# Score matmuls over all 128 rows of the key tile instead of 64

## The chip, the cores and the metric

The kernel runs on one core of a Trainium2 chip. TensorE multiplies matrices; VectorE, ScalarE and GpSimd work on what it leaves in PSUM and on SBUF; SyncE and the others issue DMAs. The metric is device time in microseconds, here the median of the runs of the kernel. A matmul has a stationary operand, which a weight load puts into the 128 by 128 array (rows are the contraction, columns the outputs), and a moving operand, which streams through it. In the profile PE is the matmuls, PEld the weight loads, DVE VectorE, ACT ScalarE, POOL GpSimd and SP SyncE.

## The reference

Attention with pooled keys and values, then a feed-forward layer with a maximum over three products.

```python
# q, k, v: (8, 8, 576, 64): batch, heads, sequence, head size
k_p = k.reshape(B, H, 72, 8, D).mean(axis=3)
v_p = v.reshape(B, H, 72, 8, D).mean(axis=3)
scores = q @ k_p^T / sqrt(D)              # 576 x 72 a head
attn = exp(scores - max); attn = attn / (attn.sum() + 1e-9)
x = (attn @ v_p), heads side by side      # 4608 x 512
h = maximum(maximum(x @ w1, x @ w2), x @ w3)   # 4608 x 768
out = h @ w_out                           # 4608 x 512
```

The change touches only the product of queries and pooled keys.

## The kernel before

The eight batches flow through the kernel as a pipeline: while the feed-forward layer works on the tokens of one batch, the attention of a later one is made. Tokens are taken 512 at a time by the feed-forward layer (stage n is tokens 512n to 512n + 511) and 576 at a time by a batch of the attention.

Feed-forward. The kernel uses max(a, b, c) = a + max(0, b - a, c - a): it subtracts w1 from w2 and w3 once, makes the two products x(w2 - w1) and x(w3 - w1) (`hidden_part`, line 362, tile `pw`), takes the relu of the first on ScalarE (line 368) and the maximum with the second on VectorE (line 370), and adds x(w1 w_out) to the output (`project`, lines 412 and 416, tile `po`). Each `pw` is four matmuls of 512 columns. Later stages make such products with seven instead of eight block products (`seven`, line 789; `out_seven`, line 713).

Attention of a batch b. GpSimd adds groups of eight keys and values (lines 161 to 164). Queries are transposed, on TensorE (`turn_q`, line 192) or by a DMA (step `T`, line 302), into `qTs[b]`, a tile of 128 rows: a block of 128 columns of the queries holds two groups of the 64 head dimensions, so the even group lies in rows 0 to 63 and the odd one in rows 64 to 127. The pooled keys are transposed too (`keys`, line 199), and lines 208 to 211 copy them twice: into `kz_all[b % 2][0]`, where they fill rows 0 to 63, and into `kz_all[b % 2][1]`, where they fill rows 64 to 127. The other 64 rows of both tiles are zero from memsets at the start (lines 142 and 319). VectorE makes these copies, and ScalarE those of `kz_all[..][1]` for batches above 2.

`score` (line 213) multiplies one head's keys with a strip of its queries; `f % 2` says whether the strip lies in the upper or the lower rows, and picks the matching key tile. `scores` (line 228) makes a head of batches 1 to 6 with two such calls: 320 columns into one PSUM bank and 256 into the next. Since `tp` differs by one, one of the two has the upper rows and the other the lower. An exponential on ScalarE (line 223) then reads both. The PSUM tile has two buffers, so the scores of one head wait for the exponential two heads before. Batch 0 (`scores4`, `scores2`) and batch 7 (`scores_flat`) cut the strips differently; there `len(pools)` is 1 and 3.

The order of the work on each engine is the order of the calls, written by hand. `block(0, ...)` (line 810) sets batch 1 among the first stage: slots 26 to 30 hold its scores, alone or two heads together. `MIDDLE` (line 881) is the order of stages 1 to 4 and holds the scores of batches 2 to 5, such as "h s0 h s1 h s2": `h` is one `pw` of four matmuls, `s0` the scores of head 0. `LEAD` (line 531) does the same for batch 6, and `ORDER` (line 846) for batch 7. `v0` to `v4` in these strings are the products with the values (line 268) for 128 tokens each, `x0` to `x4` the transposes of their results, `k` the key copies.

Lines 215 to 220 are the ones to follow:

Of the kernel before, what the change touches and what calls it, by code (L numbers as in the profile page):

```python
# [14 lines left out]
def kernel(  # L15
# [44 lines left out]
    pools = [first.enter_context(tc.tile_pool(name="ps0", bufs=1, space=PSUM))]  # L60
# [152 lines left out]
    def score(b, h, out, tp, i0, i1):  # L213

        f = NG * (h // 2) + tp
        n = f // 2
        rows = slice(0, 128) if len(pools) != 2 else slice(64 * (f % 2), 64 * (f % 2) + 64)
        nc.tensor.matmul(out, kz_all[b % 2][f % 2][rows, h, :],  # L218
                         qTs[b][rows, n + i0:n + i1, 64 * (h % 2):64 * (h % 2) + 64],
                         start=True, stop=True)  # L220
# [7 lines left out]
    def scores(b, h):  # L228
        psc = psum([128, 1024], F32, name="psc", tag="att", bufs=2)
        score(b, h, psc[:, 192:512], 0, 0, 5)  # L230
        score(b, h, psc[:, 512:768], 1, 0, 4)
        exp(ets[b][:, h, :], psc[0:Sp, 192:768])

    def scores_flat(b, j):

        psc = psum([128, 512], F32, name="psf", tag=SC[0], bufs=SC[1])
        u = 8 * j
        while u < 8 * j + 8:
            h, t = divmod(u, NG)
            tp, i0 = divmod(t, 5)  # L240
            n = min(5 - tp - i0, 8 * j + 8 - u)
            at = 64 * (u - 8 * j)
            score(b, h, psc[:, at:at + 64 * n], tp, i0, i0 + n)
            u += n
        exp(ets[b].rearrange("p h s -> p (h s)")[:, 512 * j:512 * j + 512], psc[0:Sp])
# [734 lines left out]
```

## Time and profile before

| | before |
|---|---|
| time, median of 3 runs | 230.57 us (230.28 to 230.62) |
| span of the profiled execution | 228.6 us |
| TensorE matmuls busy | 219.2 us, 96% |
| weight loads busy | 138.6 us, 61% |
| VectorE busy | 149.1 us, 65% |
| ScalarE busy | 122.3 us, 53% |
| GpSimd busy | 138.7 us, 61% |

The page gives the profiled execution by its span alone, from the first to the last instruction; the times of the runs are those of the whole execution on the device. Matmuls are pipelined: one starts while the last columns of another are still on their way, and the end of each is modelled. So the sum of their durations is not what they cost; the distance from one start to the next is. The mean granted clock of TensorE is 0.998 of full speed.

In a line of a group, "64*128" is the part of the array in use (rows by columns), "64x320 bf16" the operand, then the count, the busy time, the mean duration in ns, and the idle time just before, with what ended it. In the timeline the first column is the start and the second the duration of a merged group, both in us.

### The profile page before, as it was taken

Reading aid. Unit: us, or ns where it says so; the run is one execution under the profiler, and the core shown is the slowest. Engines: PE = TensorE matmul, PEld = TensorE weight load, DVE = VectorE, ACT = ScalarE, POOL = GpSimd, SP = SyncE. Lnnn points to the kernel's source line nnn. Section 1 sums busy time; section 2 is a strip of 40 time slices with the busy share of each in tenths; the row PEclk is TensorE's granted clock in tenths of the full one; section 3 lists DMA queues with packets and bytes.
Section 4 is the critical chain, followed back from the end, with each engine's and each line's share of the span. In section 5 each row is a group of like instructions: output and inputs, shape, how many; then the busy total and the mean of one; then the engine's idle time right before and its main releaser. Section 6 shows DMA issues by size and latency. Waiting matters only on the chain.

```text
span 228.6 us, 4690 instructions
## 1 busy us (share of the span) xinstructions
PE 219.2 (96%) x1806; PEld 138.6 (61%) x1807; DVE 149.1 (65%) x292; ACT 122.3 (53%) x221; POOL 138.7 (61%) x111
## 2 busy tenths in 40 slices
PE   7788999999999999999999999899999999999993
PEld 2477745369436533973396349534678677788882
DVE  3668875048465374876487558635668896898841
ACT  2277425746864477237623762575587545555330
POOL 7975202999959766687668755999600923773020
PEclk9999999999999999999999999999999999999999
DMA  6999999999569999359999996761351434200265
GB/s 181 211 196 196 212 203 208 192 189 221 107 106 212 224 211 199 61 123 164 220 205 168 167 250 113 155 171 51 50 128 26 106 67 106 46 3 0 47 208 163
DMA packets 47351, 33.54 MB, mean 147 GB/s; under 512 B 27041, under 2 KB 42337, under 8 KB 47329
## 3 DMA queue, kind: packets, MB, share of 16 engines
q0 software_dynamic: 16944, 16.98, 45.6%
q1 hardware_dynamic: 29936, 15.87, 29.7%
q10 hardware_dynamic: 448, 0.39, 0.7%
q8 instruction: 14, 0.23, 0.4%
q14 instruction: 9, 0.07, 0.1%
HBM read 34.60 MB, written 9.44 MB: 193 GB/s over the span
## 4 chain that ended last, share of the span: by engine, by line
PE 88%; DMA 4%; DVE 3%; ACT 2%; issue 1%; SPq 0%; ACTq 0%
PE pw L362 28%; PE po L416 9%; PE oA L713 9%; PE pA L789 7%; PE po L412 6%; PE psc L218 5%; PE oC L713 4%; PE pav L268 4%; PE pC L789 3%; DMA ktTrue<-in_k_dram 3%; PE oB L713 2%; PE pm L349 2%; PE pqt L192 2%; PE pB L789 2%; PE pxt L259 2%; DMA xT<-xn 1%
## 5 line engine op out<-in xcount | busy, mean ns | idle before, releaser
L362 PE MATMUL pw<-xT,mw 128*128 128x512 f16 (+1 forms) x336 | 73.1, 350 | 0.3 <-ACT xT L262 0.2
L370 DVE TENSOR_TENSOR hT<-t,pw 128x512 f16<-128x512 f16 (+1 forms) x42 | 25.5, 610 | 27.4 <-PE pw L362 25.0
L362 PEld LDWEIGHTS <-mw 128*128 128x128 f16 x336 | 28.6, 97 | 23.9 <-issue 0.6
L223 ACT ACTIVATE et<-psc 72x576 f16<-72x576 f32 (+2 forms) x54 | 35.1, 661 | 8.4 <-PE psc L218 8.2
L161 POOL TENSOR_TENSOR half<-vt 72x2048 f32<-72x2048 f16 x7 | 28.4, 4059 | 13.3 <-DMA vt<-in_v_dram 12.8
L162 POOL TENSOR_TENSOR half<-half 72x1024 f32<-72x1024 f32 (+1 forms) x13 | 27.2, 2096 | 12.2 <-DVE rcp L274 7.3
L368 ACT ACTIVATE t<-pw 128x512 f16<-128x512 f32 (+1 forms) x42 | 22.5, 537 | 16.6 <-PE pw L362 16.1
L276 DVE TENSOR_TENSOR xn<-pav,rcp 128x512 f16<-128x512 f32 x40 | 27.7, 692 | 1.4
L416 PE MATMUL po<-mwo,hT 128*128 128x512 f16 (+1 forms) x102 | 23.5, 367 | 0.0
L161 POOL TENSOR_TENSOR half<-ktFalse 96x1536 f32<-96x1536 f16 x6 | 18.8, 3128 | 5.2 <-issue 5.1
L218 PEld LDWEIGHTS <-kz 64*128 64x128 bf16 (+1 forms) x143 | 8.4, 94 | 21.7 <-issue 17.8
L564 POOL TENSOR_TENSOR pad<-xT 128x256 f16<-128x256 f16 x8 | 6.7, 835 | 21.4 <-ACT pad L795 13.4
L795 ACT CAST pad<-pA 128x512 f16<-128x512 f32 x27 | 15.6, 588 | 7.2 <-PE pA L789 7.0
L218 PE MATMUL psc<-qT,kz 64*128 64x320 bf16 (+3 forms) x120 | 17.7, 283 | 1.2 <-DVE qT L194 0.9
L274 DVE RECIPROCAL rcp<-pav 128x8 f32<-128x8 f32 x40 | 8.1, 203 | 14.9 <-PE pav L268 14.6
L723 ACT COPY osb<-oA 128x512 f32<-128x512 f32 x12 | 7.0, 586 | 19.5 <-PE oA L713 19.5
L268 PEld LDWEIGHTS <-et 72*128 72x128 f16 x320 | 15.2, 98 | 3.5 <-issue 0.2
L412 PE MATMUL po<-wm,xT 128*128 128x512 f16 (+1 forms) x68 | 16.6, 367 | 0.0
L268 PE MATMUL pav<-vp,et 72*128 72x65 f16 x320 | 16.4, 194 | 0.1
L769 DVE SCALAR_TENSOR_TENSOR hT<-pad 128x512 f16<-128x512 f16 x18 | 14.6, 825 | 2.1 <-ACT pad L799 1.7
L421 ACT COPY osb<-po 128x512 f32<-128x512 f32 (+1 forms) x16 | 9.2, 573 | 12.3 <-PE po L416 11.6
L789 PEld LDWEIGHTS <-sw 128*128 128x128 f16 x144 | 13.7, 98 | 2.4
(122 smaller groups left out, 377.8 us busy)
## 6 DMA issues: line engine op xcount, KB each, us to landing
out_dram<-osb SPq DMA_DIRECT2D x38, 128.0 KB, 5.2
ktFalse<-in_k_dram POOLq DMA_DIRECT2D x7, 576.0 KB, 6.9
qb<-in_q_dram POOLq DMA_DIRECT2D x7, 576.0 KB, 10.4
vt<-in_v_dram POOLq DMA_DIRECT2D x7, 576.0 KB, 14.6
mw<-in_moe_w_dram POOLq DMA_DIRECT2D x9, 256.0 KB, 9.3
out_dram<-osb SPq DMA_DIRECT2D x8, 256.0 KB, 5.9
ktTrue<-in_k_dram SPq DMA_DIRECT2D x3, 384.0 KB, 4.9
out_dram<-ob SPq DMA_DIRECT2D x8, 128.0 KB, 2.7
```

Source lines behind the costliest of these rows:

```text
L161: yield e.tensor_tensor(out=f, in0=t[:, :, 0:4, :], in1=t[:, :, 4:8, :], op=ALU.add)
L162: yield e.tensor_tensor(out=f[:, :, 0:2, :], in0=f[:, :, 0:2, :], in1=f[:, :, 2:4, :], op=ALU.add)
L218: nc.tensor.matmul(out, kz_all[b % 2][f % 2][rows, h, :], qTs[b][rows, n + i0:n + i1, 64 * (h % 2):64 * (h % 2) + 64], start=True, stop=True)
L223: nc.scalar.activation(out=out, in_=in_, func=FT.Exp, scale=1.0 / 64.0)
L268: nc.tensor.matmul(pav[:, h // 4, 65 * (h % 4):65 * (h % 4) + 65], ets[b][:, h, c0:c0 + 128], vp_all[:, b, h, :], start=True, stop=True)
L276: nc.vector.tensor_tensor(out=xn, in0=pv[:, :, :, 0:D], in1=rcp.to_broadcast([128, 2, 4, D]), op=ALU.mult)
L362: mm = nc.tensor.matmul(pw, w_sb[wi][:, kc, bass.ts(jc, 128)], x[:, kc], start=(kc == 0), stop=(kc == KCH - 1))
L370: nc.vector.tensor_tensor(out=hT[:, jc, c0:c1], in0=t, in1=pw, op=ALU.max)
L412: nc.tensor.matmul(po, tokens(128 * m, 128 * m + 128)[:, kc], wm_sb[:, kc, c], start=(kc == 0), stop=False)
L416: nc.tensor.matmul(po, hT[:, jc, bass.ts(mm, 128)], wo_sb[:, jc, c], start=False, stop=(jc == JCH - 1))
L713: nc.tensor.matmul(p, left, right, stop=(r == 4), skip_group_check=True, start=(i in FIRST and r == 0 and (m == 0 or n == LAST)))
L789: mm = nc.tensor.matmul(p[:, w], a[:, kc, bass.ts(g, 128)], b[:, kc, :], start=(i in FIRST and w + kc == 0), stop=(w + kc == 2), skip_grou ...
```

## The change

`rows` in `score` is the range of partitions that the matmul reads of both operands. Before, it is all 128 for batches 0 and 7 and the 64 rows that hold the head for batches 1 to 6. After, it is all 128 for every batch. The 64 rows that come in hold zeros in the key tile, so the products are the same.

```diff
         f = NG * (h // 2) + tp
         n = f // 2
-        rows = slice(0, 128) if len(pools) != 2 else slice(64 * (f % 2), 64 * (f % 2) + 64)
+        rows = slice(0, 128)
         nc.tensor.matmul(out, kz_all[b % 2][f % 2][rows, h, :],
                          qTs[b][rows, n + i0:n + i1, 64 * (h % 2):64 * (h % 2) + 64],
                          start=True, stop=True)
```

## The prediction

> **What bounds the kernel now.** I read the page first, for the bound, then its groups for the edited line, then the timeline of TensorE around those matmuls, then the same line where it already works with all 128 rows.
>
> ```profile
> span 228.6 us, 4690 instructions
> PE 219.2 (96%) x1806; PEld 138.6 (61%) x1807; DVE 149.1 (65%) x292; ACT 122.3 (53%) x221; POOL 138.7 (61%) x111
> PE 88%; DMA 4%; DVE 3%; ACT 2%; issue 1%; SPq 0%; ACTq 0%
> L218 PEld LDWEIGHTS <-kz 64*128 64x128 bf16 (+1 forms) x143 | 8.4, 94 | 21.7 <-issue 17.8
> ```
>
> TensorE is busy for 96% of the span and makes 88% of the chain that ended last, so a shorter TensorE stream is worth its length unless something else takes over. The last line is the clue: the weight loads of line 218 are the only frequent ones before which the loader idles long and for no work that the profile names. The same form by shape, all of TensorE:
>
> ```profile
> L218 PE MATMUL psc<-qT,kz 64*128 64x320 bf16 x48 | 14.3, 306 | 0.2 <-ACT et L223 0.2
> L218 PE MATMUL psc<-qT,kz 64*128 64x256 bf16 x48 | 13.1, 279 | 0.2 <-ACT kz L208 0.2
> ```
>
> So 96 matmuls change, 48 pairs (six batches, eight heads). They wait for nearly nothing. Their durations say little, as matmuls overlap; what a pair costs is the distance between starts. Timeline of TensorE, starts in the first column:
>
> ```profile
> 61.30 0.31 PE L218 MATMUL psc<-qT,kz 64*128 64x320 bf16 x2
> 61.54 1.04 PE L362 MATMUL pw<-xT,mw 128*128 128x512 f16 x4
> 62.51 0.31 PE L218 MATMUL psc<-qT,kz 64*128 64x320 bf16 x2
> 62.75 1.04 PE L362 MATMUL pw<-xT,mw 128*128 128x512 f16 x4
> 63.72 0.31 PE L218 MATMUL psc<-qT,kz 64*128 64x320 bf16 x2
> ```
>
> Two things are to be seen. Two matmuls together take 0.31 us, no longer than one of them (306 ns): the two halves of the array work at the same time. And four 512-column matmuls stand between, which need less than the time given to them. Their own pace, without scores, is in the chain in order of time:
>
> ```profile
> 101.65 2.59 PE pw L362 x12
> ```
>
> 2.59 / 12 = 0.216 us each, four 0.863. The period from one pair to the next is 62.51 - 61.30 = 1.21 (1.208 over 61.30 to 66.14), so a pair really costs 1.208 - 0.863 = 0.345 us. At 0.43 ns a column (0.44 us for 1024 columns, next fence) its longer half needs only 0.14 us. Of the rest, about 0.10 lies ahead (61.54 + 0.863 = 62.40, but the pair starts at 62.51) and 0.11 behind (62.51 + 0.14 = 62.65, but the next starts at 62.75): the array empties when it goes to 64 rows and again when it comes back.
>
> The batches whose scores already use 128 rows:
>
> ```profile
> 168.81 0.60 PE L218 MATMUL psf<-qT,kz 128*128 128x256 bf16 x5
> 169.25 0.42 PE L268 MATMUL pav<-vp,et 72*128 72x65 f16 x8
> ...
> 171.69 0.38 PE L218 MATMUL psf<-qT,kz 128*128 128x256 bf16 x2
> 171.91 0.60 PE L789 MATMUL pA<-pad,sw 128*128 128x256 f16 x4
> ```
>
> Five matmuls with 256 + 256 + 64 + 256 + 192 = 1024 columns take 169.25 - 168.81 = 0.44 us from start to start, two of 256 take 0.22: 0.43 ns a column, between neighbours of other types, with nothing lost ahead or behind. (The 72-row matmuls of line 268 follow without loss too, so it is not any count under 128 that empties the array.)
>
> **The change part by part.** Only the row range moves. No instruction is added or removed and no queue is touched; the keys' other 64 rows are zeros written once by the memsets of lines 142 and 319, done before 30 us, so the wider read adds no late wait; both halves of the query tile are written by the same copies or the same DMA transpose.
>
> *Lost: the two halves no longer overlap.* 320 + 256 = 576 columns at 0.43 ns are 0.247 us in place of 0.14 us: 0.107 us a pair, 48 x 0.107 = 5.1 us if nothing came back.
>
> *Gained: both gaps go.* 0.10 + 0.11 a pair. Net 0.345 - 0.247 = 0.098, called 0.10, a gain. The full-row pair is bounded by 0.247 (batch 7's pace) and, if one weight load of 97 ns a pair stood bare, 0.344, which is no gain at all; I take 0.247, because the rows of 168.81 are the same line, type and width, and there even a 64-column matmul hides the next load.
>
> The row of 61.30 agrees with a rule of the Trainium skill, page "TensorEngine Tiling (Array Packing)", section "Key Properties": a change of the tiling mode, other than of the tile, drains TensorE. Against the change speaks the page "TensorE: Matmul & The Clock Gate", Part 3, "What picks the tile position" and the goals behind it: matmuls of few rows in different row groups run concurrently, and one of them alone takes as long as one of 128 rows. This trace agrees with both; by the second alone the change would lose the 5.1 us, by both it wins 0.10 us a pair.
>
> *Sum.* Batches 2 to 6 have 40 pairs. 39 stand alone between 128-row matmuls as at 61.30: 3.9 us. At 147.2 the second half of batch 6's first pair waits for a copy of the keys on ScalarE until 147.69; there only the gap behind it goes, 0.11. Batch 1, 38 to 47 us, is different. Its first pair too waits for a key copy (VectorE, to 38.80) and gains the gap behind, 0.11; s3 at 42.02 is a lone pair, 0.10; s1 with s2 and s4 with s5 are issued as four matmuls that overlap and pay the gaps once, 0.46 us against 2 x 0.247 = 0.49: a loss of 0.03 each at most; for s6 and s7 the latter waits for ScalarE's exponential, and 0.11 behind it is won. Sum for batch 1: 0.11 + 0.10 - 0.06 + 0.11 = 0.26. All: 3.9 + 0.11 + 0.26 = 4.3 us.
>
> *Does it reach the end?* From 157 us to the last matmul TensorE has no gap of note, so what is won before is a plain shift. Before, ScalarE could be late next: in a stretch of scores it does two exponentials of 0.65 and one relu of 0.60, 1.90 us in two periods of 2.42, which become 2.22: 0.32 left. An exponential ends some 1.25 us after its pair starts, and its buffer is wanted two periods on: 2.42 before, 2.22 after. VectorE's slack is larger (5.1 of 9.2 us busy from 103.8 to 113.0). POOL runs without a break from 139.36 to 164.18; its keys of batch 7 are ready at 156.27 and read at 160.34, 4.1 us of cover against 4.2 us won by then. If POOL did not move, 0.1 us would be lost; it was released at 139.36 by VectorE, which moves too. Loads are issued some 20 us ahead of their use. I cost all this at nothing, and keep 1 us for it in the range. The short waits outside the scores (by the distance of starts 0.3 us each at 98.3, 120.8, 143.3, and 0.6 at 145.0) are for ScalarE or VectorE right behind TensorE's own work, and move along.
>
> The profiled execution has a span of 228.6 us; the median of the runs is 230.57, 2.0 above, which I take for the work around the span and leave alone. 228.6 - 4.3 = 224.3, and with 2.0 again **226.3 us**.
>
> **The rivals.**
> Slower: *the gaps stay and the halves come one after the other.* If the gaps came from the score's own start (its waits, the type change, the buffer) and not from the row count, each pair would cost 0.345 + 0.107 and the kernel 230.6 + 5.1 = 235.7 us. The point that decides is 0.107 us: more than half of the 0.21 us of gaps would have to remain. For it: most of these pairs carry a wait on ScalarE. Against: batch 7's scores carry such waits too and lose nothing, and the gap has one size at pairs with and without waits. The page's second rule above leads here if the drain is overlooked. 5 in 100.
>
> *A weight load stands bare* (the upper bound above): 0.344 a pair, nothing won, 230.5 us. For it: the loader idles 0.42 us before each of these loads today. Against: the same line hides its loads at 168.81. 2 in 100.
>
> *Half is absorbed.* ScalarE, POOL or a transfer paces a few stages: DMA engines are full in the stretches 81.0 to 90.6 and 126.5 to 135.7 (share 1.13 and 1.10), and POOL's cover at 160 us is as long as the gain. With half of 4.3 lost, 228.4. Against: TensorE waits there for none of them, and POOL idles 1 to 3 us several times a stage until 139 us. 11 in 100.
>
> *More comes than I count*: the shifted stages shorten the waits of 0.3 to 0.6 us named above, together 1.5 us; half of that gives 225.5. 5 in 100.
>
> **How the numbers follow.** The forecast, 226.3 within half a microsecond or so, has 77 in 100. Its own working gives 225.9 to 226.7 (0.09 to 0.11 a pair); absorbed waits of up to 1 us lift the end to 227.4, and a little less waiting lowers the other to 225.6. Left out are the slower case, the bare load, most of the absorbed case and part of the last, near 2 in 10. About 0.2% (0.46 us) is what measurements of this kernel can tell from no change, as its three runs span 0.34. Faster by more: 77 + 11 + 5 = 93, less one for an absorption that is almost whole, 92; within it, 3; slower, 5.
>
> **What the changed profile would show.** Right: line 218 has no 64*128 form left; the period of the score stretch falls from 1.21 to 1.11 us with the four matmuls between still at 0.863; the loader's idle time before line 218 shrinks from 17.8 us to little; the span is near 224.3. Wrong: a period that stays at 1.21 with a wait on ScalarE or VectorE ahead of the pair (absorbed), one of 1.31 with the 0.1 us gaps still there (slower), or new idle time of TensorE at 145 or 160 us for POOL or a transpose.

## The result, and the profile after

The changed kernel took 227.75 us (median of four executions, 226.4 to 228.01) against 230.52 before; the ratio is 0.9866, 95% interval 0.9836 to 0.9895. It is faster, but by 2.8 us where 4.3 were forecast, and above the stated range. The four executions were 228.01, 227.5, 226.4 and 228.0 us: one of them is the forecast, three are not. The profiled one is the slowest, with a span of 226.3 us. Its mean granted clock and those of the second and third are 1.0, that of the fourth is 0.992; by an estimate, 0.8% of its 226.2 us is up to 1.8 us, as much as it lost, so its loss need not be that of the profiled one.

Page of the changed kernel, span, busy time and chain, and its line 218:

```profile
span 226.3 us, 4691 instructions
PE 214.7 (95%) x1807; PEld 146.4 (65%) x1807; DVE 148.6 (66%) x292; ACT 122.3 (54%) x221; POOL 138.6 (61%) x111
PE 69%; DMA 15%; POOL 11%; issue 1%; DVE 1%; ACT 1%; POOLq 0%
L218 PEld LDWEIGHTS <-kz 128*128 128x128 bf16 x143 | 13.1, 98 | 13.3 <-ACT qT L194 1.1
L218 PE MATMUL psc<-qT,kz 128*128 128x320 bf16 x48 | 14.2, 299 | 0.1
```

Timeline of TensorE in the stretch that the prediction showed:

```profile
61.40 0.41 PE L218 MATMUL psc<-qT,kz 128*128 128x320 bf16 x2
61.65 1.03 PE L362 MATMUL pw<-xT,mw 128*128 128x512 f16 x4
62.51 0.41 PE L218 MATMUL psc<-qT,kz 128*128 128x320 bf16 x2
62.75 1.03 PE L362 MATMUL pw<-xT,mw 128*128 128x512 f16 x4
63.62 0.41 PE L218 MATMUL psc<-qT,kz 128*128 128x320 bf16 x2
```

The two matmuls of a pair now follow each other (0.41 us together instead of 0.31), and the next work starts 0.245 us behind the pair's start with nothing lost ahead. The period is 1.108 us instead of 1.208 (61.40 to 65.83, four periods): 0.100 us a pair, in all 32 pairs of batches 2 to 5. The weight loads of line 218 had 21.7 us of idle time before them, 17.8 without a named cause; they now have 13.3 (ahead of a pair 0.12 us instead of 0.42). TensorE did what was forecast. But the chain is now 69% TensorE instead of 88%, and DMA and GpSimd have 26%. Two pieces of the chain, start and length in us, show where it leaves TensorE:

```profile
54.43 1.00 POOL kp L164
138.71 6.32 DMA xT<-xn
```

From the first one back, the chain runs over GpSimd's sums of keys and values and the loads ahead of them, which is most of the 26%. The second one costs more. It is in the timeline of TensorE between batches 5 and 6, first before the change, then after:

```profile
145.56 0.82 PE L713 MATMUL oC<-mwo,tt 128*128 128x256 f16 x6
146.22 1.03 PE L362 MATMUL pw<-xT,mw 128*128 128x512 f16 x4
```

```profile
142.32 0.60 PE L713 MATMUL oC<-wm,tt 128*128 128x256 f16 x4
142.76 0.82 PE L713 MATMUL oC<-mwo,tt 128*128 128x256 f16 x6
145.17 1.02 PE L362 MATMUL pw<-xT,mw 128*128 128x512 f16 x4 [1.59 <-DMA xT<-xn]
```

Before, the product with `xT`, the transposed results of batch 5, follows the output matmuls at once. After, ten output matmuls start at 142.32 and need 1.09 us; the product could begin at 143.41 and begins at 145.17, 1.76 us late, when the DMA transpose has landed. The same matmuls stand one against the other in both traces, so the gain can be followed (start after, minus start of the same matmul before, in us; the three columns behind are other profiled executions of the unaltered changed kernel, further down):

| after | first shown | again | again2 | again3 |
|---|---|---|---|---|
| the common part, before any changed matmul (37.4) | +0.22 | +0.05 | +0.11 | +0.17 |
| the scores of batch 1 (51.1) | +0.09 | -0.08 | -0.02 | +0.04 |
| the key transposes of batch 2 (57.9) | +0.39 | -0.08 | -0.02 | +0.05 |
| the scores of batches 2 to 5 (135.4) | -2.80 | -3.27 | -3.21 | -3.15 |
| the wait for `xT` (146.2) | -1.05 | -3.27 | -3.22 | -3.15 |
| the scores of batch 6 (156.4) | -2.33 | -4.07 | -4.02 | -3.95 |
| the last matmul (224.5) | -2.34 | -4.03 | -3.98 | -3.92 |

Rows 2, 4 and 6, each against the row above it, are the change: 0.13, 3.2 and 0.80 us in every column but one. Rows 3 and 5 are data that came late in the execution shown first: 0.30 and 1.75 us. Its row 6 has 1.28 in place of 0.80, as batch 6's first pair, which used to wait for a copy of the keys, finds it done behind the long wait: that gives back 0.48, so the long wait costs 1.27 us net.

### The profile page after: what moved, and what is told of

Same layout as the page of the kernel before. It is cut to its first block, busy times and chain, and to the rows that moved or that the text cites. A ratio compares the mean times of both kernels' runs of the same rounds, so it can differ in the third digit from the quotient of the medians.

```text
span 226.3 us, 4691 instructions
## 1 busy us (share of the span) xinstructions
PE 214.7 (95%) x1807; PEld 146.4 (65%) x1807; DVE 148.6 (66%) x292; ACT 122.3 (54%) x221; POOL 138.6 (61%) x111
## 4 chain that ended last, share of the span: by engine, by line
PE 69%; DMA 15%; POOL 11%; issue 1%; DVE 1%; ACT 1%; POOLq 0%
PE pw L362 21%; PE oA L713 9%; DMA vt<-in_v_dram 8%; PE pA L789 7%; PE po L416 7%; PE po L412 5%; PE oC L713 4%; PE psc L218 4%; DMA mw<-in_moe_w_dram 4%; PE pC L789 3%; POOL half L161 3%; DMA xT<-xn 3%; PE pav L268 3%; PE oB L713 2%; POOL half L162 2%; PE pB L789 2%
## 5 line engine op out<-in xcount | busy, mean ns | idle before, releaser
L362 PEld LDWEIGHTS <-mw 128*128 128x128 f16 x336 | 31.6, 98 | 22.3 <-DMA xT<-xn 1.8
L370 DVE TENSOR_TENSOR hT<-t,pw 128x512 f16<-128x512 f16 (+1 forms) x42 | 25.4, 609 | 25.1 <-ACT et L223 17.8
L161 POOL TENSOR_TENSOR half<-vt 72x2048 f32<-72x2048 f16 x7 | 28.4, 4061 | 13.8 <-DMA vt<-in_v_dram 13.3
L218 PE MATMUL psc<-qT,kz 128*128 128x320 bf16 (+2 forms) x120 | 22.4, 278 | 0.8 <-DVE qT L194 0.6
L218 PEld LDWEIGHTS <-kz 128*128 128x128 bf16 x143 | 13.1, 98 | 13.3 <-ACT qT L194 1.1
L564 POOL TENSOR_TENSOR pad<-xT 128x256 f16<-128x256 f16 x8 | 5.9, 732 | 22.5 <-ACT pad L795 13.9
L766 DVE TENSOR_TENSOR pad<-pad,pC 128x512 f16<-128x512 f16 x18 | 12.3, 685 | 3.9 <-PE pC L789 3.6
```

The source lines that it names most:

```text
L161: yield e.tensor_tensor(out=f, in0=t[:, :, 0:4, :], in1=t[:, :, 4:8, :], op=ALU.add)
L218: nc.tensor.matmul(out, kz_all[b % 2][f % 2][rows, h, :], qTs[b][rows, n + i0:n + i1, 64 * (h % 2):64 * (h % 2) + 64], start=True, stop=True)
L362: mm = nc.tensor.matmul(pw, w_sb[wi][:, kc, bass.ts(jc, 128)], x[:, kc], start=(kc == 0), stop=(kc == KCH - 1))
L370: nc.vector.tensor_tensor(out=hT[:, jc, c0:c1], in0=t, in1=pw, op=ALU.max)
```

## The experiments

Two theories were open. A: the transpose is late because it shares the DMA engines with batch 7's loads, which the shorter stages have moved closer to it; how close differs from execution to execution. B: the transposes can't come earlier whatever TensorE does. And for the score pair itself: is it the change of the row mode that costs the 0.1 us twice, or the start of a score?

### The changed kernel once more

No edit.

> The changed kernel once more, unaltered. The profiled execution lost 1.76 us of its gain in one place: TensorE waits at 145.2 us for the transpose of batch 5's second 128 tokens (xT), which took 6.3 us to land where the kernel before had 3.2. Theory A (collision): that transpose shares the DMA engines with batch 7's loads and batch 7's query transpose, which the shorter stages have moved closer together; whether it is late differs from execution to execution. Then the runs spread from 226.3 (no wait) to 228.0, median 227 to 227.8, and the profile shows the wait at 145 in proportion to its time. Theory B (fixed floor): the transposes cannot come earlier whatever TensorE does; then all runs lie at 227.5 to 228.0. Both: each score pair costs 0.245 us.

Measured: 226.41 us (226.34, 226.17, 227.34, 226.47), ratio 0.9825 (0.9807 to 0.9844). Page and timeline of this execution:

```profile
span 224.6 us, 4690 instructions
PE 87%; DVE 4%; DMA 3%; ACT 2%; issue 1%; SPq 0%; ACTq 0%
...
142.29 0.82 PE L713 MATMUL oC<-mwo,tt 128*128 128x256 f16 x6
142.95 1.03 PE L362 MATMUL pw<-xT,mw 128*128 128x512 f16 x4
```

The product follows with no wait, and TensorE has its 87% back. B is out: the same program reaches 226.2 to 226.5. Two further sets of the unaltered kernel:

> The changed kernel unaltered, for more executions and a third profile. The two sets so far: 228.01, 227.5, 226.4, 228.0 and 226.34, 226.17, 227.34, 226.47. If the late transposes are a matter of chance in each execution, again a mix of 226.2 to 226.5 and of 227.2 to 228.0, with TensorE's wait at 145 us or elsewhere in the profile when the profiled one is slow, and no such wait when it is at 226.4.

> The changed kernel unaltered, beside the next two on one chip: a mix of 226.2 to 226.5 and of 227.0 to 228.0; median 226.4 to 227.

again2 gave 226.36, 227.08, 226.38, 227.02; again3 226.43, 226.23, 226.93, 226.33. All sixteen executions together: nine at 226.17 to 226.47, five at 226.93 to 227.50, two at 228.0; median 226.45. The kernel before lies at 230.1 to 231.0 beside them, with one of 232.0 among fifty-nine, whose granted clock was 0.991. The three profiled executions here were at 226.3 to 226.4, and have neither of the late rows of the table, as A expects.

### One half in the other row mode

The kernel before, with all 128 rows for the first matmul of each pair and 64 for the second:

```diff
-        rows = slice(0, 128) if len(pools) != 2 else slice(64 * (f % 2), 64 * (f % 2) + 64)
+        rows = slice(0, 128) if len(pools) != 2 or tp == 0 else slice(64 * (f % 2), 64 * (f % 2) + 64)
```

> The kernel before, with all 128 rows for the first matmul of each pair (320 columns) and 64 rows for the second (256 columns). Tells the price of the change of row mode apart from the overlap of the halves. If the 0.10 us ahead and behind belong to the change of row mode, a pair costs 0.136 + 0.10 + 0.107 + 0.10 + 0.01 = 0.45 us in place of 0.345, and the kernel gains nothing and loses 40 x 0.11 = 4 to 5 us: 234.5 to 235.5. If they belong to the start of a score (its wait, its type), the pair costs at most 0.35 and the time stays at 230.5.

Measured: 235.73 us (235.6 to 236.06), ratio 1.0224 (1.0211 to 1.0238), 5.0 us slower than the kernel before and 0.2 us above the range expected. Timeline of TensorE:

```profile
83.88 0.51 PE L218 MATMUL psc<-qT,kz 128*128 128x320 bf16 x2
84.32 1.04 PE L362 MATMUL pw<-xT,mw 128*128 128x512 f16 x4
85.19 0.51 PE L218 MATMUL psc<-qT,kz 128*128 128x320 bf16 x2
```

The period is 1.318 us and the pair costs 0.455 with the matmuls between at 0.863. By the starts nothing is lost ahead of the first, 128-row matmul, 0.096 is lost between the two, and 0.10 behind the 64-row one. So the gaps belong to the row mode and to no other trait of a score. Three ways of one pair then stand side by side: 64 and 64 rows 0.345, 128 and 64 rows 0.455, 128 and 128 rows 0.245 us.

### The change by parts

Batch 6 alone (`or b == 6` behind `len(pools) != 2`), and batches 1 to 5 alone (`or b < 6`):

> All 128 rows for batch 6 alone (from 147 us on), 64 for batches 1 to 5. Seven pairs at 0.10 and one at 0.11: 0.8 us less than the kernel before, 229.7 to 229.9, under every theory. Theory A (the shorter stages before 145 us bring transposes and loads together): the stages before 145 are as they were, so the spread stays that of the kernel before, 0.7 us or less. Theory C (the spread has nothing to do with those stages): a spread of 1 to 1.8 us here too.

> All 128 rows for batches 1 to 5, 64 for batch 6. Gains 32 x 0.10 + 0.1 to 0.2 = 3.4 us where no transpose is late: 227.2 to 227.3. Theory A: with the stages before 145 us shortened as in the changed kernel, some executions are 1 to 1.5 us slower, up to 228.7. Theory C: as much spread as in the run for batch 6 alone.

Measured: batch 6 alone 229.68 us (229.53 to 229.94) against 230.59 before, ratio 0.9962 (0.9949 to 0.9976): 0.9 us. Batches 1 to 5 alone 227.29 us (227.05 to 227.62), ratio 0.9856 (0.9843 to 0.987): 3.3 us. The parts add up to 4.2, what the undisturbed executions of the whole gain. Neither set had an execution more than 0.6 us above its fastest, so on the spread they don't decide between A and C.

### Which partner makes the transpose late

In the first, the query transpose of batch 7 is moved out of the stretch; in the second, the load of batch 7's values is left out, and batch 7 uses the values of batch 6 (its output is another). Lines of code that are cut end in "...".

```diff
-            1 v0 x0 2 v1 x1 7:T 6 7 v2 x2 5 v3 x3 v4 x4 3 6:k 4 v6+2 k7+3 v7+3
+            1 v0 x0 2 v1 x1 6 7 v2 x2 5 v3 x3 v4 x4 7:T 3 6:k 4 v6+2 k7+3 v7+3
```

```diff
-            h k k7< q7< v7< h a1 a3 a2 a4 ...
+            h k k7< q7< h a1 a3 a2 a4 ...
...
-                folding[what, b] = fold_steps(nc.gpsimd, vts[b], vp_all[:, b, :, 0:D])
+                folding[what, b] = fold_steps(nc.gpsimd, vts[min(b, 6)], vp_all[:, b, :, 0:D])
```

> The changed kernel with the DMA transpose of batch 7's queries put behind the five transposes of batch 5's values instead of between the second and the third. Theory A1 (the query transpose is the partner of the collision): the wait at 145 us goes, 226.3 to 226.6. Theory A2 (batch 7's loads are the partner): the wait stays, 227.5 to 228. Theory B: 227.5 to 228.

> The changed kernel without the load of batch 7's values (0.58 MB in SBUF); batch 7 uses those of batch 6, so this part of the output is another. Everything else is kept. Theory A2 (the loads are the partner): the loads end about 4 us earlier, before the transposes of batch 5 begin, the wait at 145 us goes, and every run is at 226.2 to 226.5, with little spread. Theory A1 or B: 227.5 to 228.

Measured: t7_late 226.86 us (226.57, 227.28, 226.02, 226.41, 227.95, 227.15), no_v7 226.42 us (226.42, 226.16, 227.75, 226.55, 226.3). As the unaltered kernel mostly isn't late either, these say little: both still have an execution near 227.8, so neither partner alone is behind all of the late ones. The way to decide is to make the suspected overlap certain:

```diff
-            h k k7< q7< v7< h a1 a3 a2 a4 f ! v5+2 h h s0 ...
+            h k h a1 a3 a2 a4 f ! v5+2 k7< q7< v7< h h s0 ...
```

> The changed kernel with batch 7's three loads issued behind the next fold step on GpSimd, about 7 us later, so that they are certain to run beside the transposes of batch 5 at 137 to 145 us. Theory A (a transpose beside a load is late): the wait at 145 us, which came in 1 of 4 profiled executions, is there in every one, 1 to 4 us long: 227.5 to 230. Rival (the wait was a chance stall that needs no load): 226.2 to 227.3 with a rare 228.

Measured: 227.45 us, all five executions at 227.12 to 227.59. A had expected 227.5 to 230 and its rival at most 227.3, so the times alone lie between the two. Timeline of TensorE:

```profile
142.37 0.82 PE L713 MATMUL oC<-mwo,tt 128*128 128x256 f16 x6
144.58 1.02 PE L362 MATMUL pw<-xT,mw 128*128 128x512 f16 x4 [1.39 <-DMA xT<-xn]
```

The same wait in the same place, 1.56 us by the starts, and a kernel 1 us slower than the unaltered one. The DMA packets of the traces (a packet is a piece in which a transfer is moved) show the condition. Columns: end of the last packet of batch 7's loads, issue of batch 5's first two transposes, and the longest time from issue to landing of `xT` from 134 us on; before_both is a version of the kernel before, described below.

| execution | loads end | transposes issued | longest landing | wait at 145 |
|---|---|---|---|---|
| before | 140.3 | 140.1, 141.5 | 4.2 | none |
| again | 139.2 | 136.8, 138.2 | 4.7 | none |
| again2 | 138.6 | 136.9, 138.3 | 4.3 | none |
| no_v7 | 133.2 | 136.9, 138.3 | 4.8 | none |
| first shown | 143.8 | 137.3, 138.7 | 7.3 | 1.76 |
| loads_late | 141.8 | 137.2, 138.7 | 6.8 | 1.56 |
| before_both | 147.4 | 141.2, 142.5 | 7.3 | 1.83, at 149 |

SyncE's queue shows how the delay passes on (first the execution shown first, then again):

```profile
137.28 2.69 SPq L253 DMA_TRANSPOSE xT<-xn  x2
140.08 4.94 SPq L302 DMA_TRANSPOSE qT<-qb  x1
145.55 3.85 SPq L253 DMA_TRANSPOSE xT<-xn  x3
```

```profile
136.81 3.64 SPq L253 DMA_TRANSPOSE xT<-xn  x2
140.56 1.93 SPq L302 DMA_TRANSPOSE qT<-qb  x1
143.02 3.80 SPq L253 DMA_TRANSPOSE xT<-xn  x3
```

Loads that end up to about 1 us behind the second transpose's issue do no harm; 3 us or more behind, they do. The ten traces that the table leaves out agree: their loads end between 3.5 us ahead and 0.7 us behind, and none has this wait. Landings of up to 4.8 us are no sign of the loads: no_v7 has them 3.7 us after its last load packet. Before the change the loads ended 1.2 us ahead of the second transpose. A stage is 0.8 us shorter now, and the loads issued at its start run on DMA time (15.9 us from the first issue to the last packet before, 17.3, 16.7 and 16.1 in again, again2 and again3): the margin went from +1.2 to -1.0, -0.3 and +0.2 us. So the shorter stages took the margin, but by themselves not enough of it for a wait.

In the execution shown first, the loads were held up besides: fifteen of their first packets, begun at 124.4 to 124.6 us, took 4.6 to 5.2 us each. Of all the other traces only one has packets of over 4 us behind 40 us: before_both, with fifteen of 5.7 to 6.3 us at the same point of the program, and the same wait. So the stall needs no change of the scores. What causes it is open, and so is whether the shorter stages make it likelier: of the sixteen executions two lie 1.6 us above the median, both in the first set, and of the fifty-nine of the kernel before one lies 1.5 above. Only one of the three has a trace; the other two have granted clocks of 0.992 and 0.991, where those of all other executions of the two kernels that are on record are 0.996 to 1.0, so they may have lost their time in another way. A is shown for the wait (a transpose beside loads that end late), not for what makes the loads late.

### The second late place

Row 3 of the table is a wait for the pooled keys of batch 2. The next edit moves the transpose at 138 us ahead of an output product, and happened to meet this one in its profile:

```diff
-            1 v0 x0 2 v1 x1 7:T ...
+            1 v0 x0 v1 x1 2 7:T ...
```

> The changed kernel with the second product with the values (v1) and its transpose of batch 5 put ahead of the output product 2, so that the transpose that TensorE waited for at 145 us is issued 1.1 us earlier. If that wait is what makes the slow executions slow, they lose at most 0.7 us in place of 1.8: all within 226.2 to 227.1. If other places make them slow too, the spread stays up to 228.

Measured: 226.47 us (227.03, 226.47, 226.47, 226.32, and one of 233.85 at a granted clock of 0.983 that nothing explains), no faster than the unaltered kernel. Timeline of TensorE of the profiled execution (227.03), and of again:

```profile
55.70 0.30 PE L199 MATMUL pkt<-ident,kp 96*128 96x96 bf16 x3 [0.15 <-POOL kp L164]
```

```profile
55.02 0.29 PE L199 MATMUL pkt<-ident,kp 96*128 96x96 bf16 x3
```

GpSimd folds batch 1's values (adds their groups of eight) when they land, issues three loads, folds batch 2's keys; TensorE reads these 16.1 us after the first fold began, or later. Folds begun at 38.5 to 38.8 us cost nothing, those at 39.15, 39.40 and 39.64 put TensorE at 55.23, 55.48 and 55.70. That load is issued some 18 us ahead of the first changed matmul, so the change does not make it late; of the gain this takes up to 0.7 us, in this trace about half of it already at 47.5 us, where TensorE reads batch 1's values. That explains executions of 227.0 to 227.1, not those of 227.3 to 228. The remedy looked plain: fold the keys first.

```diff
+    fold_k(2, nc.gpsimd)
     load_k(3, nc.gpsimd)
     load_v(3, nc.gpsimd)
     load_q(3)
-    fold_k(2, nc.gpsimd)
```

> The changed kernel with GpSimd folding the keys of batch 2 before it issues the three loads of batch 3 (2.2 us earlier). In the profiles so far TensorE reads these keys at 55.0 to 55.1 us when the first fold of batch 1's values starts by 38.8, and 16.05 us after that start when it comes later (39.30, 39.40, 39.64 give 55.36, 55.48, 55.70): up to 0.6 us. If this is what makes the 227.0 to 227.3 executions, they go, and what is left is 226.2 to 226.5 and the rare late transpose at 145 us (up to 228). If the 227 executions come from elsewhere, the spread stays as it was.

> Keys of batch 2 first, and v1 of batch 5 ahead of the output product 2: both places have more slack. If these two waits are the whole loss, all executions lie at 226.1 to 226.6, median 226.3.

> The same two moves in the kernel before, as a control. If they only take away waits for late data, the kernel before, which rarely meets them, gains 0 to 0.3 us: 230.3 to 230.6. If they are a gain of their own, more.

Measured: keys_first 228.55 us (227.6 to 229.81, and one of 232.18 at a granted clock of 0.990), both 229.47 (227.92 to 229.91), before_both 231.38 (231.0 to 232.85, and one of 243.49 at 0.979; 230.48 before on the same chip, ratio 1.0038, 1.002 to 1.0055). All three expectations missed. The wait for the keys at 55 us is gone: in the traces of both and before_both, whose first fold began as late as 39.5 us, TensorE reads them at 55.41 without a wait. (In keys_first it began at 38.2, which costs nothing anyway.) But a longer wait stands a stage later. Timeline of TensorE of keys_first, and of its GpSimd:

```profile
78.36 0.30 PE L199 MATMUL pkt<-ident,kp 96*128 96x96 bf16 x3 [0.71 <-POOL kp L164]
70.08 0.77 POOL L100 DMA_DIRECT2D qb<-in_q_dram  x1 [7.91 <-DMA qT<-qb]
```

The loads of batch 3 are issued 5.7 us later than in again. Its queries land 4.3 us later (65.4), so does their transpose (69.5), and GpSimd, which waits for it to issue the next load, folds batch 3's keys 4.2 us later (72.25 instead of 68.04). A transpose of results is late further on as well (0.83 us at 100.8). The control is of use for A: the profile of before_both, whose scores have 64 rows as ever, has the stalled packets at 127 us and the wait of the first execution shown, 1.83 us by the starts:

```profile
149.17 1.02 PE L362 MATMUL pw<-xT,mw 128*128 128x512 f16 x4 [1.67 <-DMA xT<-xn]
```

Last, more slack ahead of 145 us by an earlier load of batch 7's queries, whose buffer is free by then; q7_v1 has the edit of v1_early besides:

```diff
-            h s6 h s7 h b2 b3 b4 ! k5+2 v5+1
+            h s6 h s7 h b2 b3 b4 q7< ! k5+2 v5+1
...
-            h k k7< q7< v7< h a1 a3 a2 a4 ...
+            h k k7< v7< h a1 a3 a2 a4 ...
```

> The changed kernel with the load of batch 7's queries issued about 10 us earlier, at the end of the stage before, where its buffer is already free. Batch 7's other two loads then end some 3 us earlier, near 136 us, before the transposes of batch 5 begin. Theory A: the wait at 145 us cannot come; 226.2 to 226.5, with 227 at most from batch 1's values. Against it: the same load now runs beside the transposes of batch 4 at 115 to 122 us; if those become late, a new wait of up to 1.5 us stands at 121 us, in every execution, and the time is 227 to 228.

> The same with v1 of batch 5 ahead of the output product 2, which issues the transpose at 138 us 1.1 us earlier. Theory A: as q7_early, 226.2 to 226.5. If slow executions of 227.5 to 228 remain in both, they do not come from the wait at 145 us.

Measured: q7_early 228.11 us (227.95 to 231.36), q7_v1 229.99 (227.88 to 231.26), where again3 on the same chip had 226.38. The price that was named against it came true and was larger than the 1.5 us named: the load runs beside batch 4's transposes, and the wait stands one stage earlier. It is 1.6 us by the starts in the trace of q7_v1, of its fastest execution, and 3.2 in that of q7_early, of its slowest (231.36). Timeline of TensorE of q7_early, and its stretches (us, busy time of each engine, granted clock, DMA share, GB/s):

```profile
123.91 1.32 PE L362 MATMUL pw<-xT,mw 128*128 128x512 f16 x4 [3.08 <-DMA xT<-xn]
```

```profile
123.90:128.20 4.30, 4.29 (x15) 1.85 (x16) 1.88 (x4) 1.55 (x3) 1.41 (x2) 0.60 1.47 179
128.20:132.00 3.80, 3.80 (x22) 1.96 (x20) 2.61 (x7) 2.55 (x5) 2.01 (x1) 1.00 0.94 123
```

No version tried is faster than the changed kernel as it is.

## Why the prediction was right or wrong

*The pair's price: right.* 0.245 us against 0.247, a gain of 0.100 against 0.098; the loads of weights stay hidden, and both gaps go. one_half shows the reason given (the row mode) and rules out the slower rival's (the start of a score). The rule that a change of the tiling mode drains TensorE (the Trainium skill, "TensorEngine Tiling (Array Packing)", "Key Properties") agrees with these runs: 0.096 us ahead and 0.10 behind 64 rows, nothing at 128.

*Batches 2 to 6: right.* 3.2 + 0.80 against 3.9 + 0.11. *Batch 1: too much,* 0.13 against 0.26. The term for s6 and s7 was mis-sized: 0.11 was forecast and nothing came. The 0.07 us that s6 gains ahead of it goes into s7's wait for an exponential, which moves only with the stream before it. Behind s7 the gap of 0.11 goes, but the two halves of s7 ran at the same time, so their overlap of 0.107 goes too, and this the prediction left out.

*The sum of the undisturbed kernel:* 4.1 against 4.3; 226.2 to 226.5 in nine of sixteen executions. *The step that failed* is "Loads are issued some 20 us ahead of their use. I cost all this at nothing, and keep 1 us for it in the range." It measured each load against its own use and found cover. It didn't ask which other transfers a load runs beside. The profile before had the answer: batch 7's loads ended at 140.3 us and batch 5's transposes were issued at 140.1 and 141.5, 4.7 us ahead of the product that needs them, with landings of 2.5 to 4.2. At the slowest landing the cover was 0.5 us. The chain that ended last before the change already ran through the second of them:

```profile
141.52 3.20 DMA xT<-xn
```

When the loads ended late, the wait cost 1.75 us (1.27 net), and the 0.3 us at batch 2's keys, on GpSimd's chain ahead of the stages that were examined, came on top: 1.6 us, what the profiled execution lacks. Idle time of TensorE at 145 us for a transpose was among the prediction's own signs of being wrong. This is shown for that one execution. The median of 227.75 lies between two others, 227.5 and 228.0, which have no trace; what they lost their time to stays open. The stall behind the late loads also comes without the change, so part of the miss is chance; that nothing stood in the sum for a late transfer is not. It is the rival "half is absorbed" (228.4) by its size and, as to "a transfer", by its kind. Of the four sets of the unaltered kernel one lies there, so nothing shows its 11 in 100 to be far off. The range reached 1.1 us above the forecast, less than a wait of 1.75.

## What to carry to other kernels

Two half-height matmuls at the same time are worth it only if the time they overlap exceeds the cost of entering and leaving the mode: here 0.107 us of overlap against 0.21 us of gaps for a lone pair, while two heads in one group (0.46 and 0.48 us in 64 rows against 0.49 in 128) already paid. When TensorE gets faster in a pipeline of stages, list each transfer whose landing a matmul waits for, and which longer loads run beside it: their distance in DMA time shrinks with the stage, though each load still meets its own use. Loads were moved twice to make room (batch 3's three in keys_first, batch 7's queries in q7_early), and both times the wait moved to another stage.

## What the runs showed of the hardware that was not expected

A wait has a second price. In q7_early TensorE stood idle for 3.2 us, and then the granted clock was 0.60 in the next 4.3 us: matmuls of 512 columns started 0.427 us apart instead of 0.216, and 1.7 us more were lost. After the waits of 1.6 and 1.8 us at 145 the clock stayed full. The Trainium skill, "TensorE: Matmul & The Clock Gate", Part 1, has the clock halve after an idle window of about 3.4 us; 3.2 us sufficed here. And stalls of 4.6 to 6.3 us held fifteen load packets at once, in two traces of seventeen; their cause is open.
